# Output weights by column halves in a two-problem attention block

## The chip, the cores and the metric

The kernel runs on one core of one Trainium2 chip. A core has a matrix engine (TensorE, PE in the profile, with its weight loads shown apart as PEld), VectorE (DVE), ScalarE (ACT), GpSimd (POOL) and SyncE (SP), which here only issues transfers to the core's DMA engines. The metric is the device time of one execution in microseconds; lower is better. Before the change it is 728.03 us (median of 3 runs, 727.68 to 728.79).

## What is computed

Two independent problems A and B of the same shapes, each a grouped-query attention over a given key and value cache, followed by an output projection. Their outputs stand side by side.

```python
B, Sq, D = 16, 80, 576
Hq, Hkv, Sk, Dh = 32, 16, 512, 128          # bfloat16
def ref(x, k_cache, v_cache, wq, wo):
    q = (x @ wq).reshape(B, Sq, Hq, Dh).transpose(0, 2, 1, 3)
    k = jnp.repeat(k_cache, 2, axis=1)
    v = jnp.repeat(v_cache, 2, axis=1)
    scores = jnp.einsum("bhqd,bhkd->bhqk", q, k) * (Dh ** -0.5)
    o = jnp.einsum("bhqk,bhkd->bhqd", softmax(scores), v)
    return o.transpose(0, 2, 1, 3).reshape(B, Sq, Hq * Dh) @ wo
out = jnp.concatenate([ref(A...), ref(B...)], axis=-1)   # 16 x 80 x 1152
```

## The kernel before

**Tiling.** A unit is one batch entry with four key heads, that is eight query heads: an octet is the eight query heads over eight batch entries. There are 128 units, numbered U in the order in which they are worked on. Problem A comes first. Within a problem the octets come in pairs (`hh`, sixteen heads, `HH = 16`), and within a pair the batch comes in two halves (`half`), so that a stage of 32 units (one `prob`, one `hh`) holds sixteen heads of all 1280 rows. Two neighbouring units are the same batch entry in the two octets of the pair.

For each unit:

- TensorE projects queries (`em_qp`, L538, four matmuls of 320 columns, and the tail of the contraction, 576 - 512 rows, `em_qt`, L551). This runs 12 units ahead.
- TensorE forms scores: four blocks of 128 query rows (`em_qk`, L670, 512 columns each) and the residual 32 rows of each group (`em_qkr`, L657, four narrow matmuls per unit, two units together).
- VectorE takes each row's negated maximum (L679), ScalarE the exponential with its row sum (L683), VectorE the reciprocal (L689), GpSimd scales the row (L692).
- TensorE transposes the probabilities (`em_tr`, L724, 40 small matmuls, with the projection's tail ahead of them), and VectorE or ScalarE copies them out of PSUM into `pT` (L735 to L744).
- TensorE multiplies by V (`em_pv`, L767, four matmuls per key head), and VectorE or ScalarE copies the result into `oT` (L781), which holds a stage's attention output with the heads' width on the partitions.

**Output projection.** For each stage there are 20 output tiles: ten row tiles of 128 rows by two column halves of `DC = 288` (`NOC = 2`). An output tile is 16 matmuls into one PSUM bank, one per head, issued as two operations of eight (`em_op`, L816, `OPSPLIT = 2`), here called half tiles. In a problem's first stage the tile is copied to `acc` (L827); in the second it is added to `acc` into `osb` (L844) and stored (L850).

The output weights of a stage (`wo`, 2048 rows by 576) are loaded by SP in four transfers of four heads each (`em_ldwo`, L592), into one of four slots of `wo_sb`. All four go to one semaphore (`d_wo`). Each half tile reads all four slots and the `oT` of both octets:

```python
ot_reads = [R(("oT", half, b_, q_, pr_), ver) for b_ in bls for q_ in range(2) for pr_ in range(2)]
...
reads=ot_reads + [R(("wo", c_ % NWS), c_) for c_ in range(ci0, ci0 + NWC)]
```

**Order.** The kernel doesn't leave the order of its 5256 operations to a scheduler at run time. Every operation is registered with an engine, a key, what it reads and what it writes; operations of a kind form a stream (scores, PV, output half tiles `P`, K loads, `wo` loads and so on, 41 of them), in the order of their keys. The text `ORDER` then merges the streams: each letter takes the next operation of a stream, a quote mark ahead of it gives a copy out of PSUM to ScalarE and not to VectorE, and the digits behind it name the PSUM banks (0 to 7) that it takes. That merged order is the program order of every engine, and dependencies between engines become semaphore waits (`finalize`). So TensorE, VectorE, ScalarE, GpSimd and SP each run a fixed list and wait at its head.

**Queues and buffers.** All loads and stores stand in SP's list: K (L623, one transposing transfer for two units, three buffers of two units), V (L627, six buffers of one unit), `wq` and its tail (L503, L507), `wo` (L592), x and the stores of the output (L850, two buffers). A transfer at the head of SP's list that waits for its buffer holds back all that stand behind it. A K load waits for the last scores of the two units that used its buffer, a V load for the last PV, a `wo` load for the last half tile that read its slot, a store for its addition on VectorE.

Of the kernel before, what the change touches and what calls it, by code (L numbers as in the profile page):

```python
# [14 lines left out]
NK = 6  # L15
# [5 lines left out]
ILV = 0  # L21
VK = 8.0
KK = 8.0
NQ = 2
NWS = 4
NOC = 2
NOSB = 2
NWARM = 8
NWC = 4
# [19 lines left out]
OPSPLIT = 2  # L49
# [13 lines left out]
nEKni7KHHHHHNHj3j4IMj5Nj6MIMId3Ik4d5ILIk2dd4aBAd1dd3'ABEj5d4dd7AMd1LBdd3'Bd4dd6'ABAd2dd3BMd4Aadd5Ad6d'ABe0e1'B  # L63
oe2e7d3old4oldoe0'Bf6olf1d4p'AKe5ld2homKdpe3d7alod6lCBudAe0md2Cuoe5le4Ood1u'Boldvf36Alud0BlCd7Cpu'Adpv'Ag1245B
mue0we7'zouj1j3'yd5MulhMk4d1xhmoj3adMe0'BLe2log1346Cluc7xoe3'Acuoc0le5wolj1e2'yoe3'ze4oclc6CcMu'sof15lutd7lpvj
2e0lMc3pFcme2Fd4Cov'th'sog13FulCFue6xld0houa'BCe2'wCyd4'zu'Aoumg13ulc7ye5Oluok6c'wzuf12'Alxc0vpc'se3p'tc5e7'Bc
Lmoc0d4mse1oe6lce2Ctd5ulod3uColg07volb1uzluwe7y'Ad6oe2g04xlCBubo'yu'zCe0'xvc7ochc4u'shqc'wb5'BauAllf17e2pe6bCp
mvoc3mue0d1t'quCd7oluog45lulcxc6sc'w'Be2Ce0u'tod3'yvd6olzg47uh'Ahlc5hze1'wca'xo'ye0d7'Bsle2Ce6ouc4'Acoluf15tc3
lCcpud4'spmug02omvc3Czc'yue1e5'toe2ule0b3o'wlxod6lbBole1'qc4oe2lae5cold3Ac0locg17'tlf02z'se5'wCb4'yxuCp'A'Bvpe
1md6uoc7mchCuCe0o'sc3he2lvoche7hlbtuaolud3olug15'quf02y'zue4lpe5b1'wCCmxuod7'Bup'Ae0d3luoc6oculbv'sle6g45o'qCb  # L70
1uwlzu'xA'yc0c'Be7tme6c3oche0od4lad5Colug27Csluf36z'yue0Cc2xuwcoe7'Aub'tp'Bvlod4umqe2e0oc5vlcd3o'slpg17halc5wc
z'xe2'yd0Amoe1e7c4'Boc'td3lCsuc6olce2ug45'tolf16w'yCzub7'xlpue5'Bc4mvohce2he3'Aoblholc1pd5lscd2CCtve0g34auub1'
zxomuwbyluB'Ae6e4oc3cc5ole0d2s'qCcolvd3'qe7u'tf46olug15pGlCb0hwumChCxzv'yhe7b'Bouplue1c3Acud4oe2usd5lqug37ob1y
'w'zClue0e7oame3ubolxe2lqd6Coc1u'Acoc7luce0B'tc4scle1Cod3u'tolg57vvf24yld0uwx'Ae1pd5h'zpJmg67Jo'Bc2'yze3cmCc6x
uwe7slcac4oue2'Aco'Bc1ld0ocle5td3olg67tlse1C'ye2uoe4d5'zwu'xe6olb7ohlhe1oblCCBulc2oe4v'qcAald3uof07ulg16pv'sCc
4'wzumb2p'ye0Cxmcvoe1d6'tuo'Ae7c4luoe5blCBold3JCcJvc1'scGule0hg47ou't'qf15y'xuld2Bu'wpe4'ze0ud3'AComg67uplc1z'
ycc4C'xwe7'svocmac6d1Buloe5ue3'tcoc0lud4Alsuce2o'tg67olf05y'x'wb3lp'Aze6me2ob'Bple0Ce1Co'qe7uc4acoulc3cod6vltd
2ulog03use1mb4olwe5zblxCC'Boud3hCyue1lhe2d7hov'qc5h'Aocluhg46luf01'xu'sBc2'zcupd5'thy'we7me2b6oAle0oe4c3aod7lo
blCCulcg02su'qve6'zxc3oe4'ycb2Cltvoue0we6lobuo'Aule4Cd3pu'qd5BmuCog02luf17x'zyuc6'Bhcp'wue0'Ac5slce2ohe6mc3oad
4ltcd1Colug05slupe2'zvc3Cyc'w'xe6u'td5omc3uCBd0loucg17sluf23v'wz'x'yc6BchAe1'tc7phce0Cb4omuo'sue6lbovlAe1e2lod  # L80
5e0qld7oag46plb1xmwz'Ae2o'Be3c6'yd5ole7Cobuloulce0c4lochc3se2ctd7'tholg46CCCue3'yxb0uo'w'zuBe4lAe6c7uCalcod5vq
lc2ovcd3slutf14ug27ppme6bz'wmoe1b7ylhCoe4'qvb'Aouxd5CF'quBle0Fe2uod3lFoug67FlCuf14xlwBud0'zpe2u'ye3oc7'Acumc6o
cvd5'stle1CKug67olc2'yzcc3'wp'xcle7Cd6sv'Aoe1mc2ud0Bloucc4'ste5cloe2g37'tColf14Chylvb5a'zuCp'xe2u'Be7od3mue0ol
buo'wlud2rle1Aug57pc6y'zcd0'wo'se7b5loKme6Kbo'xalCBe1v'Ad4olue2c7Crlcuog36uCtlf15xuy'wc7'zcpu'Bc3e2scvme6oc7u'
tchoe1ld3Duolhd4sk2'Apg67lLd0'x'Be1y'zc2aco'wd4mCe7u'Ac6oc'tc3luse2cClog56uCtluf17y'zue3xe2'wob5u'Aplve0hobmho
hle6pd3Dlc1hoc'Bc2rd0Dcg45thsd2zmb1y'x'w'BCAle7vc4ocue0e6loae5ubColuc7sld3uoe0crlg46Cov'tCf15'wxu'zd7p'Bu'Ae6b
3'yuolpue2blCoume0ud4loDvg16hCrle2zmc3coe0b6aslxoe5'ye3bwB'AClove1d4olue0c7olcud5Colug23rlutf16y'xhu'we7'zCDe0
ouc2'Ac'Bc3Cvplcd4shumd5oDutg27lue1w'xc3'zCpe0vc'Aac7ymucd4o'tue2'soc7lucoe6d3lsc1'Bocle0tg57olf12Club6puhCwme
0hxubo'Bu'zAe1'yrd3plDd4oe7Gg56olc0Jw'yce1'zc5c'x'sd6th'Be0loJe5b4aCmouole7vboluAd2lre0c3ocg45'slf13z'yc7xcp'B
e5d4'twlCAe2uc7Comcub6Colve0'se1uohle5d7Duolbaovlpg02ulruc1C'wC'zce6u'xtd5'Ay'Bue1d4mCoug27olue0xb3lvwo'Auze1l  # L90
e6e5uohd7yd0lobKolc2Ccr'Bue1C'sf36olug24plupc5mucc1tc'zvc3hs'xe5'wDe4'yocJd1mtGd2loJe6Bc3Klcoc5K'Ace0D'stg47la
of35'ze6lb7o'yCxle0uwe4Cob'Bu'Aplue2oe1c6mvcrd0o'sud3lpg67lCvc4zmb2uo'xu'Be7le5ocbaolCe1C'wurd3loe2ud7'Aolug05
y'tulCf14xyv'zc6c'Bue0c5'soc'wue2'tc7hod6lhAclhd5CCpuD'sg03pume2yud7'zomk1vc3Ld0lue4c'x'wao'Bg12Ale5wc6o'ycc4'
# [174 lines left out]
def bass_concat_heads__gqa_block_cached__gqa_block_cached__near_ridge_kernel(  # L268
# [27 lines left out]
    with ExitStack() as es:  # L296
# [32 lines left out]
        def R(res, ver):  # L329
            return (res, ver)  # L330
# [598 lines left out]
```

## Time and profile before

| | |
|---|---|
| time, median of 3 runs (lowest to highest) | 728.03 us (727.68 to 728.79) |
| the profiled execution's own time | 731.59 us |
| its span, from the first to the last instruction | 729.8 us |
| mean granted clock of TensorE | 0.997 |
| HBM read, written | 87.65 MB, 2.95 MB |
| output half tiles' matmuls (L816) | 1280, 287 ns each from start to modelled end |
| `wo` loads | 16 of 576 KB, landing 4.0 to 9.2 us after issue |
| K loads | 64, landing 6.1 to 13.4 us after issue |

The profile is one execution, recorded instruction by instruction. Its groups are named by engine and by line of the kernel, with what is written and read (`ps<-wo_sb,oT` writes PSUM from the weights and the attention output). Matmuls are pipelined: the duration of one overlaps the next, so their spacing is read from the starts. "Idle before" and "waits" say what an engine stood for; the chain of waits follows the last instruction back to what released it at each step. A stretch is a window of time with each engine's busy time in it.

### The profile page before, as it was taken

Reading aid. Unit: us, or ns where it says so; the run is one execution under the profiler, and the core shown is the slowest. Engines: PE = TensorE matmul, PEld = TensorE weight load, DVE = VectorE, ACT = ScalarE, POOL = GpSimd, SP = SyncE. Lnnn points to the kernel's source line nnn. Section 1 sums busy time; section 2 is a strip of 40 time slices with the busy share of each in tenths; the row PEclk is TensorE's granted clock in tenths of the full one; section 3 lists DMA queues with packets and bytes.
Section 4 is the critical chain, followed back from the end, with each engine's and each line's share of the span. In section 5 each row is a group of like instructions: output and inputs, shape, how many; then the busy total and the mean of one; then the engine's idle time right before and its main releaser. Section 6 shows DMA issues by size and latency. Waiting matters only on the chain.

```text
span 729.8 us, 26289 instructions
## 1 busy us (share of the span) xinstructions
PE 719.5 (99%) x10820; PEld 514.5 (71%) x10820; DVE 637.6 (87%) x1447; ACT 643.9 (88%) x1856; POOL 432.0 (59%) x650
## 2 busy tenths in 40 slices
PE   9999999999899999999999999999999999999998
PEld 5567777777677777777777777777777777777677
DVE  4998898998799989889898987999888998989995
ACT  1999997998879989999899998899999999898993
POOL 0466656566637546646666575665755756757772
PEclk9999999999999999999999999999999999999999
DMA  9999998989979999999899994999978989897950
GB/s 235 257 282 253 247 229 231 213 208 243 221 176 258 209 247 241 260 212 229 205 235 243 271 250 124 249 232 253 207 188 204 259 190 223 203 240 191 207 165 19
DMA packets 365976, 160.73 MB, mean 220 GB/s; under 512 B 278560, under 2 KB 362784, under 8 KB 365856
## 3 DMA queue, kind: packets, MB, share of 16 engines
q1 hardware_dynamic: 365856, 159.05, 92.6%
q8 instruction: 86, 1.41, 0.8%
q14 instruction: 34, 0.28, 0.1%
HBM read 87.65 MB, written 2.95 MB: 124 GB/s over the span
## 4 chain that ended last, share of the span: by engine, by line
PE 87%; DMA 4%; ACT 3%; DVE 3%; SPq 1%; issue 1%; POOL 1%
PE ps L816 21%; PE ps L767 18%; PE ps L538 16%; PE ps L670 14%; PE ps L724 9%; PE ps L657 4%; PE ps L551 4%; DMA kT<-in_A_k_cache_dram 3%; ACT p_sb L683 3%; DVE negmax L679 2%; DMA kT<-in_B_k_cache_dram 1%; POOL p_sb L692 1%; SPq L503 1%; SPq L507 0%; ACT pT L735 0%
## 5 line engine op out<-in xcount | busy, mean ns | idle before, releaser
L692 POOL TENSOR_SCALAR p_sb<-p_sb,rinv 128x512 bf16<-128x512 bf16 x640 | 430.2, 692 | 282.2 <-DVE rinv L689 281.8
L683 ACT ACTIVATE p_sb<-ps,negmax 128x512 bf16<-128x512 f32 x640 | 442.2, 706 | 31.6 <-DVE negmax L679 25.5
L679 DVE TENSOR_REDUCE negmax<-ps 128x1 f32<-128x512 f32 x640 | 417.3, 680 | 37.2 <-PE ps L670 29.4
L767 PE MATMUL ps<-pT,v_sb 128*128 128x160 bf16 x2048 | 187.9, 233 | 2.3 <-issue 1.9
L816 PE MATMUL ps<-wo_sb,oT 128*128 128x288 bf16 x1280 | 182.9, 287 | 0.6 <-issue 0.4
L767 PEld LDWEIGHTS ps<-pT,v_sb 128*128 128x128 bf16 x2048 | 152.8, 98 | 40.0 <-issue 5.0
L670 PE MATMUL ps<-kT,qT 128*128 128x512 bf16 x512 | 175.5, 381 | 0.5 <-DMA kT<-in_A_k_cache_dram 0.3
L538 PE MATMUL ps<-xT,wq_sb 128*128 128x320 bf16 x1024 | 174.0, 299 | 0.3 <-DVE xT L402 0.3
L816 PEld LDWEIGHTS ps<-wo_sb,oT 128*128 128x128 bf16 x1280 | 122.4, 98 | 45.6 <-ACT p_sb L683 2.7
L683 ACT ACTIVATION_READ_ACCUMULATOR p_sb<-ps,negmax 128x1 f32 x640 | 141.3, 221 | 0.0
L538 PEld LDWEIGHTS ps<-xT,wq_sb 128*128 128x128 bf16 x1024 | 95.2, 98 | 44.3 <-ACT qT L564 1.6
L724 PEld LDWEIGHTS ps<-ident,p_sb 64*128 64x128 bf16 x5120 | 91.4, 95 | 9.3 <-ACT oT L781 1.9
L724 PE MATMUL ps<-ident,p_sb 64*128 64x64 bf16 x5120 | 95.8, 190 | 1.1 <-DVE oT L781 0.6
L735 ACT COPY pT<-ps 128x512 f32<-128x512 f32 x145 | 85.2, 600 | 12.2 <-PE ps L724 11.9
L737 DVE COPY pT<-ps 128x1024 bf16<-128x1024 bf16 x111 | 75.7, 685 | 12.0 <-PE ps L724 10.6
L564 ACT ACTIVATE qT<-ps 128x320 bf16<-128x320 f32 x156 | 69.0, 454 | 17.8 <-PE ps L551 15.5
L781 DVE CAST oT<-ps 128x320 bf16<-128x320 f32 x129 | 61.6, 481 | 10.2 <-PE ps L767 9.4
L670 PEld LDWEIGHTS ps<-kT,qT 128*128 128x128 bf16 x512 | 48.3, 98 | 26.5 <-ACT p_sb L683 4.8
L781 ACT CAST oT<-ps 128x320 bf16<-128x320 f32 x127 | 54.5, 440 | 10.0 <-PE ps L767 9.8
L565 DVE TENSOR_SCALAR qT<-ps 128x320 bf16<-128x320 f32 x100 | 47.2, 480 | 6.1 <-PE ps L551 4.5
L744 DVE COPY pT<-ps 128x256 bf16<-128x256 bf16 x135 | 36.7, 281 | 12.5 <-PE ps L724 11.0
L657 PE MATMUL ps<-kT,qT 128*32 128x512 bf16 x512 | 39.6, 384 | 0.9 <-DMA kT<-in_B_k_cache_dram 0.5
(31 smaller groups left out, 191.2 us busy)
## 6 DMA issues: line engine op xcount, KB each, us to landing
v_sb<-in_A_v_cache_dram SPq DMA_DIRECT2D x64, 512.0 KB, 5.3
v_sb<-in_B_v_cache_dram SPq DMA_DIRECT2D x64, 512.0 KB, 4.8
wo_sb<-in_A_wo_dram SPq DMA_DIRECT2D x8, 576.0 KB, 6.1
wo_sb<-in_B_wo_dram SPq DMA_DIRECT2D x8, 576.0 KB, 6.6
wq_sb<-in_B_wq_dram SPq DMA_DIRECT2D x4, 1024.0 KB, 6.3
out_dram<-osb SPq DMA_DIRECT2D x40, 72.0 KB, 3.7
wq_sb<-in_A_wq_dram SPq DMA_DIRECT2D x8, 256.0 KB, 4.6
wq_sb<-in_A_wq_dram SPq DMA_DIRECT2D x2, 1024.0 KB, 6.0
```

The costliest lines, as they stand in the source:

```text
L538: last = e.matmul(ps[:, vbq[h].phys, QO:QO + 320], lhsT=wq_sb[:, wsl, ck, hi * 128:(hi + 1) * 128], rhs=xT[:, half, ck, n0:n0 + 320], star ...
L564: return e.activation(dst, src, AF.Identity, scale=SCALE)
L670: return e.matmul(ps[:, vb.phys, :], lhsT=qT[:, qsl, bl, gl * 160:gl * 160 + 128], rhs=k_of(U, gl), start=True, stop=True)
L679: return e.tensor_reduce(negmax[:, si:si + 1], ps[:, vb.phys, :], axis=AX.X, op=AluOpType.max, negate=True)
L683: return e.activation(p_sb[:, psl, :], ps[:, vb.phys, :], AF.Exp, bias=negmax[:, si:si + 1], scale=1.0, accum_out=rowsum[:, ss, k:k + 1])
L692: return e.tensor_scalar(p_sb[:, psl, :], p_sb[:, psl, :], rinv[:, ss, k:k + 1], 1.0, op0=AluOpType.mult, op1=AluOpType.mult)
L724: last = e.matmul(dst, lhsT=p_sb[64 * h:64 * h + 64, psls[k_], j * 128:(j + 1) * 128], rhs=ident[64 * h:64 * h + 64, 64 * h:64 * h + 64], ...
L735: return e.copy(pT[:, pts, :, :].bitcast(F32)[:, :, 32 * h:32 * h + 32], ps[:, vtp[h].phys, :].rearrange("p (n c) -> p n c", n=16))
L737: return e.tensor_copy(pT[:, pts, :, 64 * h:64 * h + 64], psb[:, vtp[h].phys, :].rearrange("p (n c) -> p n c", n=16))
L767: last = e.matmul(ps[:, vo.phys, off:off + 160], lhsT=v_sb[:, vs, gl, j * 128:(j + 1) * 128], rhs=pT[:, pts, 4 * gl + j, :], start=(j == 0 ...
L781: return (e.copy if en == "act" else e.tensor_copy)(dst, src)
L816: last = e.matmul(ps[:, vb.phys, 0:DC], lhsT=oT[:, hi, rb * 128:(rb + 1) * 128], rhs=wo_sb[:, wi, c3 * DC:(c3 + 1) * DC], start=(hi == 0), ...
```

## The change

**Loads.** `wo_sb` becomes four buffers of eight heads by 288 columns, one for each pair of column half (`c3`) and octet. A stage's four transfers carry the same bytes as before, each with rows of 576 bytes and not 1152, and each has a semaphore of its own. The second column half's loads get a key that is five output tiles later than the first's.

**Tiles.** Output tiles go by column half: all five row tiles of a batch half with `c3 = 0`, then the five with `c3 = 1`. The last ten tiles of all keep the old order, row tile by row tile. A half tile is now the eight heads of one octet; it reads the `oT` of that octet and the one buffer of `wo` that it needs. A lower bound on a tile's key keeps it behind the PV of its last unit.

**Order.** `ORDER` is another text for the same 5256 operations, with the same number in each stream; the keys' constants `OPX`, `LP0` and `WOK` that sort the half tiles and `wo` loads change with it. Counted by transpositions (one per unit) that stand ahead of them, the four `wo` loads of the stages stand at 2, 2, 3, 3; 34, 34, 34, 35; 66, 66, 66, 67; 98, 98, 98, 99 before, and at 1, 3, 11, 11; 33, 34, 37, 42; 65, 69, 70, 73; 97, 97, 103, 103 after. Half tiles stood in groups of two to four between transpositions with gaps (ahead of transpositions 20 to 32 by count: 20, 22, 24, 24, 24, 26, 28, 30, 32, 32, 32, 34, 36), and now 20, 22, 22, 22, 23, 24, 25, 26, 28, 28, 29, 30, 32. Of the copies out of PSUM, ScalarE had 575 and VectorE 489; now ScalarE has 563 and VectorE 501.

The K load is rewritten with a constant `KSP = 0`, with which it issues the same transfers to the same places as before. The warm-up matmuls read other views of `wo_sb` of the same size.

```diff
@@ constants @@
-NWS = 4
-NWC = 4
-OPSPLIT = 2
+KSP = 0
-OPX = ((12.0, 1.8), (18.5, 1.45), (17.5, 1.05), (8.5, 1.35))
-LP0 = 8.5
+OPX = ((7.0, 1.6), (6.7, 1.7), (9.0, 1.7), (11.0, 1.35))
+LP0 = 11.0
+WOK = 6.0
@@ ORDER: all of it @@
...
@@ buffers @@
-        wo_sb = sb("wo_sb", [128, NWS * (HH // NWC), D], BF16)
+        wo_sb = sb("wo_sb", [128, 4, HH // 2, DC], BF16)
-        warm = wo_sb[:, 0, 0:512]
-        ones = wo_sb[:, 1, 0:128]
+        warm = wo_sb[:, 0, 0:2, 0:256]
+        ones = wo_sb[:, 0, 3, 0:128]
@@ loads of wo @@
-                for wc in range(NWC):
-                    h0 = hh * HH + wc * hc
-                    ci = (prob * NPAIR + hh) * NWC + wc
-                    wos = ci % NWS
-                    x = 5.0 * (prob * UPR + hh * NPP * 16 + OPX[2 * prob + hh][0]) - WOL * (NWC - wc)
+                for wos in range(4):
+                    c3, h0 = wos // 2, hh * HH + wos % 2 * (HH // 2)
+                    ci = prob * NPAIR + hh
+                    o0_, os_ = OPX[2 * prob + hh]
+                    x = 5.0 * (prob * UPR + hh * NPP * 16 + o0_ + c3 * os_ * NRT) - WOL * (2 - wos % 2) - WOK
...
-                        src = wo_ap[h0 * 128:(h0 + hc) * 128, :]
-                        return e.dma_start(wo_sb[:, wos * hc:(wos + 1) * hc, :],
-                                           src.rearrange("(h p) n -> p h n", p=128))
+                        src = wo_ap[h0 * 128:(h0 + HH // 2) * 128, c3 * DC:(c3 + 1) * DC]
+                        return e.dma_start(wo_sb[:, wos, :, :], src.rearrange("(h p) n -> p h n", p=128))
...
-                          dsem="d_wo", name="ldwo%d.%d.%d" % (prob, hh, wc), stream="wo")
+                          dsem="d_wo%d" % wos, name="ldwo%d.%d.%d" % (prob, hh, wos), stream="wo")
@@ output tiles @@
-                        r, c3 = divmod(n, NOC)
+                        r, c3 = divmod(n, NOC) if prob == 1 and hh == NPAIR - 1 and half == NPP - 1 else (n % NRT, n // NRT)
...
+                        x = max(x, 5.0 * (base + 16 * half + 2 * bls[-1] + 1) + PV0 + 4.0)
...
-                        ot_reads = [R(("oT", half, b_, q_, pr_), ver) for b_ in bls for q_ in range(2)
-                                    for pr_ in range(2)]
+                        ot_reads = [[R(("oT", half, b_, q_, pr_), ver) for b_ in bls for pr_ in range(2)] for q_ in range(2)]
...
-                                for hi in range(sp_ * hs, (sp_ + 1) * hs):
-                                    wi = (ci0 + hi // hc) % NWS * hc + hi % hc
-                                    last = e.matmul(ps[:, vb.phys, 0:DC], lhsT=oT[:, hi, rb * 128:(rb + 1) * 128],
-                                                    rhs=wo_sb[:, wi, c3 * DC:(c3 + 1) * DC],
-                                                    start=(hi == 0), stop=(hi == HH - 1))
+                                for i in range(HH // 2):
+                                    last = e.matmul(ps[:, vb.phys, 0:DC],
+                                                    lhsT=oT[:, sp_ * (HH // 2) + i, rb * 128:(rb + 1) * 128],
+                                                    rhs=wo_sb[:, 2 * c3 + sp_, i, :],
+                                                    start=(sp_ == i == 0), stop=(sp_ == 1 and i == HH // 2 - 1))
...
-                                  reads=ot_reads + [R(("wo", c_ % NWS), c_) for c_ in range(ci0, ci0 + NWC)],
+                                  reads=ot_reads[sp_] + [R(("wo", 2 * c3 + sp_), ci)],
```

More of the change, by code (lines that the diff above doesn't have):

```diff
@@ L67 @@
[L67 to L71, printed above, removed]
@@ new lines @@
+1md3Bo'tcmg45hF'se6'yxe1hCBc7u'zFe4oclae5vb3olute0lwboolc7Ce1olud6Acluc4qcCovd3se0ulg25Cou'tf17'yxuCBe4'zd2wvp
+lc3d5uAmoe0ucpg16'sulob3wlze4A'ye6bhCouholavc2d1q'xulcd3tme0Bf26og45plpc7mcyd0'wme2sc4oc'ze7d6C'txulBc4cou'Ae5
+c3'socle1g24o'thlChCe7uxb3'who'yua'Ae2le5uoe0b'zuolCe1Bd4ulod6vloc7ue2lCqcc5ovlcg03slCtvf17y'zue2'xCb3p'Buwmpc
+6ucAbmuo'sue0le1hoc7ud4'qhold3hae2lcCovg56'tluf01y'zub7w'xCpu'Be2Ambuople0c3oc'qc4'se2d5loce7C'td3vole0ug46lub
+2'zCymohb'wJxBGe1'qc7oJcle2hc3Ald4hoe0acClod5vsg16lu'tuf27C'zwyb3u'xpuc6AmcuBe0e1oe4uc5bsloc'qd6tle0od3oe1lg25
@@ L352, in em_warmend @@
         def em_warmend(e):
-            return e.memset(warm[:, 0:2], 0.0)
+            return e.memset(warm[:, 0, 0:2], 0.0)
         S.add("dve", -1000, em_warmset, writes=[R(("warm",), 0)], name="warmset", stream="warmset")
@@ L627, in em_ldv @@
                 return e.dma_start(v_sb[:, vs, :, :], src)
-            if goct < ILV or U % 2 == 0:
+            if kw == 1 or U % 2 == 0:
                 S.add("sp", 5.0 * gfirst[U] + 0.5 * (U - gfirst[U]) - LA - KK, em_ldk,
-                      writes=[R(("kT", (U + i_) % NK), U + i_) for i_ in range(2 if goct >= ILV else 1)],
+                      writes=[R(("kT", (U + i_) % NK), U + i_) for i_ in range(kw)],
                       dsem="d_k%d" % ks, name="ldk%d" % U, stream="K")
```

148 lines of the change are left out of this document (75 added, 73 removed).

## The prediction

> **What bounds the kernel now.** I read the page first, then the gaps between matmul starts, then who waits for whom, then stretches of time, then the DMA landings. The page says that TensorE hardly pauses, at full clock, while VectorE and ScalarE are close behind and the DMA engines are nearly full:
>
> ```profile
> span 729.8 us, 26289 instructions
> ...
> PE 719.5 (99%) x10820; PEld 514.5 (71%) x10820; DVE 637.6 (87%) x1447; ACT 643.9 (88%) x1856; POOL 432.0 (59%) x650
> ...
> PEclk9999999999999999999999999999999999999999
> ...
> q1 hardware_dynamic: 365856, 159.05, 92.6%
> ```
>
> Busy time of pipelined matmuls overlaps, so 99% proves little. I therefore laid the 10820 matmuls of the trace against the order table, operation by operation: 1664 TensorE operations, from the start of each to the start of the next. Medians: an output half tile (8 matmuls, L816) 0.980 us, a head of PV (4, L767) 0.277, a score block (L670) 0.216, a head's projection (4, L538) 0.543, a pair's residual scores (8, L657) 0.548, a transposition with projection tails (42, L724 and L551) 0.825, without tails 0.690, and about 0.096 more ahead of an operation that uses part of the array. Over before's table these medians add up to 712.7 us; the trace needs 724.8 from first to last start. So 12.1 us are waits, 11.1 of them in 39 gaps of over 0.04 us, the rest jitter. They lie in four places. Under 50 us: 2.7. From 194 to 201 us: 3.7. Elsewhere to 660 us: 2.0. From 666 to 693 us: 2.7. Rows for the second and the last:
>
> ```profile
> PE ps L767 <- issue: 1.9, 1, 1.9
> ...
> 197.00:200.40 3.40, 3.40 (x19) 0.50 0.74 190
> ...
> 672.00:692.00 20.00, 18.62 (x355) 12.91 (x348) 19.75 (x48) 19.93 (x59) 15.48 (x24) 1.00 0.97 214
> ```
>
> The first row is the longest wait of TensorE's matmuls, for nothing that the profile shows; the second (stretch, PE busy, granted clock) says that half the clock followed it. I count neither against the table's order, and the timed runs seem to lack the event: 731.6 less 3.7 is 727.9, against a median of 728.03. My baseline is **727.9**. The third row (PE, weight loads, DVE, ACT, POOL busy) shows VectorE and ScalarE full for 20 us while TensorE pauses: the 2.7 us near the end are theirs. In the chain of waits, two K loads decide:
>
> ```profile
> 321.25 10.14 DMA kT<-in_A_k_cache_dram
> ...
> 596.40 9.70 DMA kT<-in_B_k_cache_dram
> ```
>
> K pairs 29 and 54 landed 0.14 us before their first score block started; TensorE stood 0.52 and 0.60 us around them. That is 1.1 of the 2.0; the other 0.9 is scattered.
>
> **The change, part by part.**
>
> *TensorE work.* Every count stays: 160 half tiles, 512 PV heads, 512 score blocks, 256 projections, 128 transpositions. The medians summed over the new table (a dozen new neighbour pairs priced by their first member) give 711.9: **-0.8**. The half tiles' matmuls have the same 288 columns, and the four wo semaphores in place of one add waits ahead of them at no price: a score block followed by a half tile takes the same 0.216 us as one followed by another score block. The warm-up reads other views of the same buffer, as large as before: 0.
>
> *First eight heads don't wait for the second octet.* This wait costs nothing today: of the idle time before L816's operations the trace puts 0.4 us, in two waits, down to a copy into oT (L781); and the shortest distance from a PV to the half tile that needs it is 0.69 us by the medians (0.92 after). **0**, at best -0.4. Its loss is bounded by banks held longer (a tile's bank is open 2.5 us in the median before, 2.9 after, 7 at most in both), which is in the distances below.
>
> *wo in column halves.* Still 16 loads of 576 KB, each row of 576 bytes and not 1152:
>
> ```profile
> wo_sb<-in_A_wo_dram SPq DMA_DIRECT2D x8, 576.0 KB, 6.1
> ...
> SPq L850 <- DVE osb L844: 39.6, 13, 12.6
> ...
> SPq L592 <- PE ps L816: 3.4, 2, 2.5
> ```
>
> In the packet records 1152 bytes take 51 ns and 576 bytes (the output stores) 29, so 16384 x 29 - 8192 x 51 is 57 us over 16 engines: 3.6 us of DMA time, 0.5% of the span. K, V and wo lie ahead of need by several us, which hides it: **0**, at worst 3.6. The Trainium skill (DMA: Bandwidth & Descriptors, Specifications) has line rate from 512 bytes up, so by it there would be no loss at all; the trace disagrees, since 576 bytes in 29 ns is 19.9 bytes per ns against 22.6. By the page the worst case here would be 0.
>
> On SP's queue a wo load waits for the last reader of its buffer with K, V, weights and stores queued behind it; K in turn waits behind stores, which stood 39.6 us at the head for their VectorE add (pair 53 was issued 0.4 us after one). Before: four wo loads in a row, 3.4 us of waiting. After, on the medians' clock, 13 us over the six that wait at all, the longest 5.4. What decides is how long before its use each K pair is issued, counting everything ahead of it on SP (4.5 us per K, 0.4 to 0.6 per other load, from SP's rows). Before: lowest 7.5 (pair 53), 9.0 (54), 10.9, 12.3 (29), 12.3. After: 10.0 (pair 60), 11.2 (62), 11.8 (63), 12.0 (56), 12.8 (34), 13.3 (40). K lands 8.1 us after issue in the middle, 9.4 to 10.1 in the waits above. So both of today's waits go and pair 60 may come just late: 1.1 becomes 0.5, **-0.6** (between -1.1 and the third case below). The wo loads themselves gain distance: first use 10.5 to 13.2 us after issue today in the last three stages, 22 to 59 after, but one at 10.3; the longest landing is 9.2.
>
> *Even output tiles.* VectorE's and ScalarE's work per 20 us of TensorE's (rows' means; 0.645 for a max and 0.67 for an exponential, as these follow one another in the chain): before, mostly 17 to 21 in each, but 25.2 and 24.4 in the last full stretch but one, just where the third row above has both full. After, the largest are 22.4 and 22.3 (600 to 620), and 22.3 and 22.8 from 40 to 60, where before has 19.0 and 19.7. The tight places near the end go: before, units 121 and 122 have 4.6 and 5.0 us from last score to transposition, and banks come round after 1.36 (scores), 0.58 and 0.65 (PV) where the waits are; after, the shortest are 5.3 (the last unit; 5.1 there before, without a wait), 1.90 and 0.76, besides a transposition's bank at 0.55. So of 2.7 I leave 0.4: **-2.3**, between -2.7 and 0. At the start I take 2.7 to 3.0, **+0.3** (0 to +3): projection work ahead of the first scores is longer (the first K landed at 18.9 us, now first needed at 18.1 by the medians plus 1.2 for the first start), but x is loaded ahead of the second K pair, which had 3.9 us to spare, and the first transposition stands 5.8 us behind its residual scores, 7.6 before. For 600 to 620 add **+0.1**. The end after the last tile (3.8 us from its first matmul) keeps its order.
>
> *Sum:* 727.9 - 0.8 - 0.6 - 2.3 + 0.3 + 0.1 = **724.6**. Waits left: 4.9 of today's 7.4 (the event at 194 us left out). No waits at all would give 727.9 - 0.8 - 7.4 = 719.7.
>
> **Rivals.**
>
> *Waits move but don't shrink.* VectorE and ScalarE carry 22 us of work per 20 in two new stretches; if the 2.4 us too much stay in each (as before's 5 too much left 2.7, a half), 2 x 1.2 comes on top, and with pair 60 late by another 0.5 it is 727.5: within 0.2% of 728.03, which is about what a measurement here can tell from none (1.5 us). For: all three engines stand within 13% of full. Against: a queue a few operations deep spreads a bump, and before's stretch of 20.5 and 23.0 at 60 to 80 us cost 0. This is also the case in which the change does not do what it says, as its third part frees nothing.
>
> *K comes late.* The second pair of wo loads now lands amid K and V, and in the last units K's distances are the shortest. K has been slower where wo loads lay beside it:
>
> ```profile
> DMA to landing us min/median/max: 6.1/8.1/13.4
> ```
>
> The 13.4 is pair 4, issued just behind four wo loads at the start. Landings as slow at 10.0, 11.2, 11.8, 12.0, 12.8 and 13.3 would cost 3.4 + 2.2 + 1.6 + 1.4 + 0.6 + 0.1 = 9.3, 8.8 over my 0.5: **733.4**, slower. It decides from 12.6 us on (2.6 + 1.4 + 0.8 + 0.6 = 5.4, which gives 729.5). Against: K lies at 6 to 10 us once the start is over, and few weights are loaded near the end. As the row at 197 us stands after a stop of 2.0 us, each stop that long may cost 1.7 more at half the clock, so two would end at 736.8. The Trainium skill (TensorE: Matmul & The Clock Gate, What's actually happening) has the clock fall only after an idle window of about 3.4 us; the trace agrees with the window's length (3.40 us at 0.50) but not with that need, as 2.0 us of idle was enough. By the page the stops alone would count: 733.4.
>
> **How the numbers follow.** Forecast 0.68, waits that move 0.20, late K 0.12. Likeliest time 724.6; its own range 721.5 to 726.6. Faster by over 0.2% means under 726.6: 0.68. Within: 0.20. Slower, over 729.5: 0.12. The range runs from 721.5 (hardly any wait left, plus jitter) to 729.3, so that the late K's upper part is left out.
>
> **What would show it.** Starts of TensorE's operations should again add up to about 712, with 5 us of waits on top. The stretch that ends 40 us before the end should have VectorE and ScalarE under 19 of 20. No K load should stand as a long piece in the chain after 60 us, except perhaps pair 60. wo rows should land in 6 to 9 us in pairs. I am wrong if waits past 2 us appear ahead of L657 or L670 on a K load, if ScalarE or VectorE is full for 20 us where TensorE pauses, or if half-tile matmuls start over 0.123 us apart.

## The result and the profile after

The changed kernel takes 722.53 us (median of 4 runs, 721.79 to 722.56) where the kernel before takes 727.93 (4 runs, 727.68 to 728.79). The ratio is 0.9921, with a 95% interval of 0.9904 to 0.9938: faster by 5.4 us in the medians, 4.5 to 7.0 by the interval. The profiled execution is one of 722.56 us. Line numbers differ from kernel to kernel: the score block, the exponential, PV, its copy and the addition into `osb` are L670, L683, L767, L781 and L844 before, L673, L686, L770, L784 and L845 after, and up to 9 lines further down than before in experiments 1, 2 and 4. The lines of the page that answer to those shown of before, with the first line of the chain of waits:

```profile
span 720.6 us, 26290 instructions
...
PE 715.3 (99%) x10820; PEld 513.1 (71%) x10820; DVE 641.3 (89%) x1459; ACT 639.8 (89%) x1844; POOL 432.6 (60%) x650
...
q1 hardware_dynamic: 374048, 159.05, 95.6%
...
PE 98%; ACT 1%; issue 0%; DVE 0%
...
wo_sb<-in_A_wo_dram SPq DMA_DIRECT2D x8, 576.0 KB, 5.6
```

The busy shares hardly move. What moved is the chain: its line gives TensorE 98% of the span, and no K load is in it. The same line of before:

```profile
PE 87%; DMA 4%; ACT 3%; DVE 3%; SPq 1%; issue 1%; POOL 1%
```

Problem A's wo lands 0.5 us sooner (6.1 before), although it comes in twice as many packets. SP's waits, the rows that answer to the two of before (total us, times, longest):

```profile
SPq L851 <- DVE osb L845: 35.1, 10, 8.9
...
SPq L590 <- PE ps L673: 9.4, 4, 4.6
```

The wo loads do stand longer at the head of SP's list (9.4 us here against 3.4). All the same, K came in time: the landings, and five stretches of time (PE, weight loads, DVE, ACT, POOL busy, the granted clock, DMA share, GB/s; a share above 1.00 means that the recorded times of packets overlap).

```profile
DMA to landing us min/median/max: 6.3/8.6/13.1
```

```profile
20.00:40.00 20.00, 19.34 (x234) 11.57 (x234) 19.91 (x46) 19.99 (x60) 11.51 (x19) 1.00 1.15 270
40.00:60.00 20.00, 20.00 (x353) 13.93 (x351) 19.98 (x47) 20.00 (x62) 14.11 (x22) 1.00 1.11 272
600.00:620.00 20.00, 20.00 (x323) 13.90 (x322) 19.50 (x42) 19.87 (x62) 13.37 (x20) 1.00 0.91 195
660.60:680.60 20.00, 20.00 (x323) 14.72 (x321) 18.68 (x43) 18.30 (x56) 16.17 (x24) 1.00 0.88 187
680.60:700.60 20.00, 20.00 (x324) 14.47 (x323) 18.79 (x45) 19.92 (x59) 13.54 (x21) 1.00 0.80 222
```

In the second and third stretch VectorE and ScalarE are as full as they were at 672 to 692 us before, and TensorE does not pause; in the first they are as full, and it does (one wait of 0.7 us at 27 us). So two full engines alone are not reason enough for a pause. The fourth is the stretch that ends 40 us before the end: both engines are under 19 of 20, as the prediction had asked. In the fifth ScalarE is full again, without a pause.

Laid against the order table as in the prediction, TensorE's operations take 715.6 us from the first start to the last (724.8 before). "Medians" is the sum of undisturbed spacings, "waits" what stands above them, by place in the kernel. The last two rows are experiments told below.

| profile | time, us | first to last start | medians | waits under 50 us | 50 to 640 | behind 640 |
|---|---|---|---|---|---|---|
| before | 731.59 | 724.8 | 712.0 | 3.3 | 5.6 | 2.7 |
| after | 722.56 | 715.6 | 711.5 | 1.2 | 1.4 | 0.0 |
| before, a quarter of V | 725.48 | 718.8 | 712.0 | 3.2 | 0.4 | 2.0 |
| after, a quarter of V | 721.42 | 714.5 | 711.5 | 1.3 | 0.2 | 0.0 |

The time is the first-to-last distance plus 6.7 to 7.0 us in each row. So the gain lies in waits, in all three places, and 0.5 us of it in spacings. Two things about the first row. Its medians are not those of the prediction: taken from before's profile alone they are 712.7, with 2.7 us of waits under 50 us, so some 0.6 us can be booked as spacing or as waits at the start (after alone has 711.3 and 1.2). And the profiled execution of before is 3.6 us above its median time, because the event at 194 us is at its longest there and half the clock follows it. Experiment 1, with the same order and bank numbers and the same time, has 2.3 us in the middle column by the same working; with that figure the waits that went are 2.1, 0.9 and 2.7 us, and with 0.5 of spacings the sum is 6.2, near the 5.4 between the medians.

### The profile page after: what moved, and what is told of

The parts are those of the page before. It is cut to its first block, busy times and chain, and to the rows that moved or that the text cites. A ratio compares the mean times of both kernels' runs of the same rounds, so it can differ in the third digit from the quotient of the medians.

```text
span 720.6 us, 26290 instructions
## 1 busy us (share of the span) xinstructions
PE 715.3 (99%) x10820; PEld 513.1 (71%) x10820; DVE 641.3 (89%) x1459; ACT 639.8 (89%) x1844; POOL 432.6 (60%) x650
## 4 chain that ended last, share of the span: by engine, by line
PE 98%; ACT 1%; issue 0%; DVE 0%
PE ps L816 22%; PE ps L770 20%; PE ps L537 19%; PE ps L673 16%; PE ps L727 11%; PE ps L660 5%; PE ps L550 4%; ACT p_sb L686 1%; PE ps L348 0%; PE ps L396 0%; ACT qT L563 0%; PE ps L414 0%; PE ps L451 0%; DVE osb L845 0%; DVE wo_sb L341 0%
## 5 line engine op out<-in xcount | busy, mean ns | idle before, releaser
L686 ACT ACTIVATE p_sb<-ps,negmax 128x512 bf16<-128x512 f32 x640 | 444.0, 711 | 29.8 <-DVE negmax L682 25.5
L770 PE MATMUL ps<-pT,v_sb 128*128 128x160 bf16 x2048 | 191.1, 233 | 0.1
L770 PEld LDWEIGHTS ps<-pT,v_sb 128*128 128x128 bf16 x2048 | 154.0, 98 | 39.5 <-ACT pT L745 3.3
L673 PE MATMUL ps<-kT,qT 128*128 128x512 bf16 x512 | 176.4, 381 | 0.0
L537 PE MATMUL ps<-xT,wq_sb 128*128 128x320 bf16 x1024 | 176.0, 299 | 0.0
L686 ACT ACTIVATION_READ_ACCUMULATOR p_sb<-ps,negmax 128x1 f32 x640 | 144.0, 225 | 0.0
L738 ACT COPY pT<-ps 128x512 f32<-128x512 f32 x150 | 88.4, 603 | 9.4 <-PE ps L727 9.0
L740 DVE COPY pT<-ps 128x1024 bf16<-128x1024 bf16 x106 | 72.0, 684 | 13.2 <-PE ps L727 11.7
L563 ACT ACTIVATE qT<-ps 128x320 bf16<-128x320 f32 x131 | 59.5, 462 | 16.2 <-PE ps L550 15.4
L784 DVE CAST oT<-ps 128x320 bf16<-128x320 f32 x129 | 61.5, 482 | 6.5 <-PE ps L770 6.0
L564 DVE TENSOR_SCALAR qT<-ps 128x320 bf16<-128x320 f32 x125 | 59.5, 482 | 8.1 <-PE ps L550 6.6
L673 PEld LDWEIGHTS ps<-kT,qT 128*128 128x128 bf16 x512 | 48.4, 97 | 25.7 <-issue 3.3
L784 ACT CAST oT<-ps 128x320 bf16<-128x320 f32 x127 | 56.4, 448 | 10.2 <-PE ps L770 9.9
L745 ACT COPY pT<-ps 128x128 f32<-128x128 f32 x132 | 36.1, 288 | 7.0 <-PE ps L727 6.8
L692 DVE RECIPROCAL rinv<-rowsum 128x3 f32<-128x3 f32 (+1 forms) x256 | 39.5, 161 | 2.3 <-ACT p_sb L686 2.2
```

Source lines behind the costliest of these rows:

```text
L537: last = e.matmul(ps[:, vbq[h].phys, QO:QO + 320], lhsT=wq_sb[:, wsl, ck, hi * 128:(hi + 1) * 128], rhs=xT[:, half, ck, n0:n0 + 320], star ...
L563: return e.activation(dst, src, AF.Identity, scale=SCALE)
L673: return e.matmul(ps[:, vb.phys, :], lhsT=qT[:, qsl, bl, gl * 160:gl * 160 + 128], rhs=k_of(U, gl), start=True, stop=True)
L686: return e.activation(p_sb[:, psl, :], ps[:, vb.phys, :], AF.Exp, bias=negmax[:, si:si + 1], scale=1.0, accum_out=rowsum[:, ss, k:k + 1])
L738: return e.copy(pT[:, pts, :, :].bitcast(F32)[:, :, 32 * h:32 * h + 32], ps[:, vtp[h].phys, :].rearrange("p (n c) -> p n c", n=16))
L740: return e.tensor_copy(pT[:, pts, :, 64 * h:64 * h + 64], psb[:, vtp[h].phys, :].rearrange("p (n c) -> p n c", n=16))
```

## The experiments

Each was timed in several rounds beside the kernel before on the same chip (728.4 to 728.7 us there).

**1. The layout alone.** Before's table to the letter, with wo in column halves, four semaphores, and half tiles that wait for both octets and all four buffers.

```diff
 # ORDER, tile order and wo keys: before's
-        wo_sb = sb("wo_sb", [128, NWS * (HH // NWC), D], BF16)
+        wo_sb = sb("wo_sb", [128, 4, HH // 2, DC], BF16)
-                                  reads=ot_reads + [R(("wo", c_ % NWS), c_) for c_ in range(ci0, ci0 + NWC)],
+                                  reads=ot_reads[0] + ot_reads[1] + [R(("wo", w_), ci) for w_ in range(4)],
```

> Before's order and tiles, with wo loaded by column halves (rows of 576 bytes) into four buffers; each half tile still waits for all four buffers and both octets. Theory (the halved rows are hidden, the gain is all in the order): same as before, 728 us within 1; wo packets 16384 of 576 bytes, DMA share up by 0.5 to 3% of the span. Rival (the separate buffers themselves help): under 726.5. Rival (the shorter rows cost DMA time that is not hidden): up to 3.6 us slower, 731.5, with K loads landing after TensorE asks for them in more than the two places of before.

Measured: 728.70 us, ratio 1.0002 (0.9988 to 1.0015). The queue's row on its page:

```profile
q1 hardware_dynamic: 374048, 159.05, 92.6%
```

The 8192 more packets are there, and the share of time is 92.6%, as before. The layout is worth nothing and costs nothing, to within 1 us.

**2. The end alone.** Before's table up to transposition 107, the changed order from there. The kernel around it has the new buffers, and each half tile reads its own octet and one buffer, as after.

```diff
 # ORDER
-<before: 128 transpositions>
+<before: to transposition 107><after: the rest>
```

> Before's order up to transposition 107, then after's order for the rest; wo by column halves, tiles row by row. Theory (VectorE and ScalarE overload near the end is 2.7 us of the gain): waits past 660 us fall from 2.7 to about 0.5, a seam at transposition 107 costs up to 0.8, TensorE's medians add up to 0.5 less: 728.0 - 2.2 - 0.5 + 0.5 = 725.8. Rival (the gain lies in the loads and the early stages): 727.5 to 728.

Measured: 728.24 us, ratio 0.9996 (0.9986 to 1.0006). The expectation missed. Waits of TensorE from 605 us on, all that the profile names:

```profile
PE ps L679 <- ACT qT L567: 0.7, 1, 0.7
PE ps L679 <- DVE qT L568: 0.5, 1, 0.5
PE ps L679 <- DVE pT L746: 0.2, 1, 0.2
```

None lies behind 640 us, so the end's 2.7 us did go. But these waits stand at 615 to 634 us, where the two orders were joined (2.3 us with the smaller ones; on the medians one bank came round there 0.2 us after its last matmul). A seam cut by hand costs as much as the thing under test, so this run decides nothing by its time.

**3. VectorE relieved at the end.** Before's kernel, with the row maximum of units 112 to 122 taken over 128 of the 512 columns.

```diff
-                def em_max(e, vb=vb, si=si):
-                    return e.tensor_reduce(negmax[:, si:si + 1], ps[:, vb.phys, :], axis=AX.X,
+                def em_max(e, vb=vb, si=si, nc_=128 if 112 <= U <= 122 else 512):
+                    return e.tensor_reduce(negmax[:, si:si + 1], ps[:, vb.phys, 0:nc_], axis=AX.X,
```

> Before, with the row maximum of units 112 to 122 taken over the first 128 of 512 score columns, which takes some 0.4 us off each of 55 VectorE operations there and leaves order, banks and ScalarE alone. Theory (VectorE full for 20 us is what holds TensorE near the end): waits past 660 us fall from 2.7 to under 1.2, time 726 to 726.8. Rival (ScalarE, equally full, or the short way round of the PSUM banks holds it): waits stay over 2, time 727.5 to 728.

Measured: 728.05 us, ratio 1.0000 (0.9988 to 1.0012). The stretch of the prediction's third row, and TensorE's waits from 660 to 700 us, of this kernel:

```profile
672.00:692.00 20.00, 18.80 (x344) 13.09 (x340) 13.51 (x48) 20.00 (x59) 15.71 (x25) 1.00 0.97 220
```

```profile
PE ps L724 <- ACT oT L781: 0.8, 2, 0.6
PE ps L816 <- issue: 0.4, 1, 0.4
PE ps L816 <- ACT p_sb L683: 0.3, 1, 0.3
```

The rows of before that answer to the first of these:

```profile
PE ps L724 <- DVE oT L781: 0.6, 1, 0.6
...
PE ps L724 <- ACT oT L781: 0.3, 1, 0.3
```

VectorE falls from 19.75 to 13.51 of 20, and the waits stay at 2.55 us (2.66), operation by operation: 0.65 ahead of transposition 120 in both. A full VectorE was not their cause. The "issue" row is told of below. What the others wait for are copies out of the banks that they take (L781 copies PV's result, L683 is a score's exponential), soon after the matmuls that filled them. The longest, ahead of transposition 120, can be followed to its end. In both kernels the transposition takes the bank of the first two PV heads of unit 118, and the copy that frees it is ScalarE's; the VectorE copy that the row of before names is of another bank and ended 0.04 us later. ScalarE in this run (start, us taken):

```profile
686.51 0.76 ACT L683 ACTIVATE p_sb<-ps,negmax 128x512 bf16<-128x512 f32 x1
...
687.17 0.51 ACT L781 CAST oT<-ps 128x320 bf16<-128x320 f32 x1
```

The bank's last matmul ended at 686.60, the copy began only behind the exponential ahead of it in ScalarE's list, and TensorE went on at 687.74, 0.06 us after the copy's end. The other waits of over 0.1 us in this stretch, the "issue" one left out, end the same way, on an operation of ScalarE's that began when the one ahead of it was done. So this run, which relieves VectorE alone, says nothing against ScalarE, which is full here too (20.00) and was relieved in no run.

**4. The start alone.** The changed order up to about transposition 4, before's from there, in the same kernel as experiment 2.

```diff
 # ORDER
-<before: 128 transpositions>
+<after: to transposition 4><before: the rest>
```

> After's order up to about transposition 4 (two wo loads there instead of four), then before's order; wo by column halves. Theory (the start is worth 1.2 us: waits before 50 us 2.7 in before, 1.5 in after, and 0.3 less in medians): 728.0 - 1.5 = 726.5, with the seam's 0 to 0.5 on top. Rival (the start is worth nothing, the difference there is one run's chance): 728.

Measured: 727.78 us, ratio 0.9989 (0.9980 to 0.9997), a smaller gain than the 726.5 expected. The waits under 52 us are 3.6 in sum, of which 1.3 (0.83 at 48.9 us, 0.48 at 51.3) are the seam; 2.3 without it, against 3.3. The gain that the ratio shows, 0.2 to 1.5 us, is the part that the seam left.

**5. The octet wait given back.** The changed kernel, each half tile waiting for both octets.

```diff
-                                  reads=ot_reads[sp_] + [R(("wo", 2 * c3 + sp_), ci)],
+                                  reads=ot_reads[0] + ot_reads[1] + [R(("wo", 2 * c3 + sp_), ci)],
 # ORDER: 22 first halves moved to just ahead of their second halves
```

> The changed kernel, in which every half tile waits again for the attention output of both octets. So that this can be met, 22 of the 80 first halves are moved to just ahead of their second halves, and PSUM banks are chosen anew there. On the medians some ten banks are then taken again 0 to 1.3 us after their last matmul, where the changed kernel has 0.76 or more. Theory: the wait of one octet for the other was worth nothing in before's order, but without its removal the changed order can't keep its bank distances; each of the ten short returns costs 0.2 to 0.7 us, together some 4 us: 726.5. Rival (the octet wait is worthless in either order): 722.5, within 0.7.

Measured: 739.88 us, 17.3 above the changed kernel and 1.0152 (1.0138 to 1.0166) of before. Waits of TensorE behind 50 us, the largest groups:

```profile
PE ps L673 <- ACT p_sb L686: 2.0, 5, 0.8
PE ps L537 <- ACT pT L738: 1.9, 3, 0.8
```

The direction was the theory's, the size four times its figure: 55 waits (20.7 us) and not ten. Where a first half of 0.98 us is taken out, everything behind it comes 0.98 us nearer to the operation whose bank it takes. Other than the expectation says, the order that ran keeps every bank number; besides the 22 moves only one copy near the end stands elsewhere. The wait and the moves were not separated, and another order might meet the wait for less.

**6. Before's end put back.** The changed kernel up to transposition 117, before's order to the end, no bank chosen anew; one store moved up.

```diff
 # ORDER
-<after: 128 transpositions>
+<after: to transposition 117><before: the rest>
```

> The changed kernel's order up to transposition 117, and before's order from there to the end; the weights' column halves stay, and no bank is chosen anew. Theory: before's waits near the end are short returns of PSUM banks written in its order (on the medians the banks of T119 come round 0.58 us after the last matmul on them, those of SR62 1.36, those of T120 0.65). So 1.8 to 2.3 us of TensorE waits come back behind 683 us, in the same places: 724.6. Rival (they come from what was queued up on VectorE and ScalarE before): no wait over 0.2 us past 683 us, 722.5.

Measured: 726.58 us, ratio 0.9968 (0.9955 to 0.9980). Waits of TensorE from 660 to 700 us, then stretches:

```profile
PE ps L770 <- DVE osb L845: 2.3, 1, 2.3
PE ps L673 <- ACT p_sb L686: 0.7, 1, 0.7
PE ps L727 <- ACT oT L784: 0.4, 1, 0.4
PE ps L727 <- DVE oT L784: 0.2, 1, 0.2
```

```profile
674.00:677.60 3.60, 1.40 (x45) 0.87 (x43) 1.00 (x4) 0.78 (x2) 0.55 (x1) 1.00 0.87 201
677.60:681.00 3.40, 3.31 (x51) 2.32 (x51) 3.10 (x10) 2.42 (x7) 2.59 (x4) 0.53 0.00 0
```

The first wait and 0.84 us just ahead of it are the seam (VectorE stood 2.6 us for a store, as two additions into one output buffer now follow closely), and half the clock for 3.4 us came behind it. The last two rows are before's short returns: transposition 120 waits 0.43 us (0.65 before), transposition 121 0.18 (0.19 before). They came back with the order, 0.6 us where the theory had 1.8 to 2.3; a sum of 2 us can't be read off this run, because the half clock lies over two of them, and the time answers to neither theory (724.6 and 722.5).

**7. Bank numbers only.** Before's order letter for letter; 289 of its bank numbers chosen so that the distance from a bank's last matmul to its next is as long as can be where it was shortest.

```diff
 # ORDER, its second line (the letters are the same)
-oe2e7d3old4oldoe0'Bf6olf1d4p'AKe5ld2homKdpe3d7alod6lCBudAe0md2Cuoe5le4Ood1u'Boldvf36Alud0BlCd7Cpu'Adpv'Ag1245B
+oe2e4d3old7oldoe0'Bf6olf1d5p'AKe2ld4homKdpe3d7alod6lCBudAe0md2Cuoe5le4Ood3u'Boldvf16Alud0BlCd7Cpu'Adpv'Ag5243B
```

> Before's kernel and order, letter for letter, with only 289 of its PSUM bank numbers chosen anew so that a bank comes round later where it came round soonest. On the medians the shortfalls against the shortest return without a wait fall from 12.8 to 5.5 us in sum (0.1 us of margin each). Near the end nothing else can be chosen (T119, SR62, T120 stay short). Theory: waits at the start shrink from 3.1-3.3 to about 2.2 and scattered ones by some 0.3; those past 660 us stay at 2.0 plus one of instruction fetch: 727.0. Rival (the numbers of banks don't matter, only which engine is full): 728.2, all waits as before.

Measured: 755.42 us, ratio 1.0368 (1.0352 to 1.0383): 27 us slower where a gain of 1 was expected. Waits of TensorE, the largest groups:

```profile
PE ps L670 <- ACT p_sb L683: 5.3, 11, 0.8
PE ps L767 <- ACT p_sb L683: 2.1, 5, 0.6
PE ps L657 <- ACT p_sb L683: 1.9, 4, 0.7
```

Neither theory had this. The shortest distances had become longer, as meant, and the waits went from 11.6 to 34.7 us in sum. They end on ScalarE's exponentials. I had taken one needed distance for all score banks, 1.95 us, near the shortest that went without a wait; but a bank is free when its copy is done, and that depends on the copy's turn in ScalarE's list. (That this is the whole reason is read from the waits; numbers chosen by the copies' ends were not tried.) With TensorE's work, the order and every engine's work the same, bank numbers alone moved 27 us.

**8 and 9. A quarter of V.** Both kernels, with V in full for the first six units only.

```diff
-            def em_ldv(e, vc_ap=vc_ap, b=b, q=q, vs=vs):
-                src = vc_ap[b, 4 * q:4 * q + 4, :, :].rearrange("g (p j) d -> p g (j d)", j=4)
-                return e.dma_start(v_sb[:, vs, :, :], src)
+            def em_ldv(e, vc_ap=vc_ap, b=b, q=q, vs=vs, w=4 if U < NV else 1):
+                src = vc_ap[b, 4 * q:4 * q + w, :, :].rearrange("g (p j) d -> p g (j d)", j=4)
+                return e.dma_start(v_sb[:, vs, 0:w, :], src)
```

> Before's kernel with V loaded in full for the first six units only, and after that only one of the four key heads' V; the other three multiply by V that an earlier unit left. This leaves out some 48 MB... that is 122 of 128 units times three quarters of 512 KB, about 46 MB of the 88 read. All engines have the same work. Theory: the long landings of K and the late instruction fetches come from full DMA queues, so the wait at 194 us (0.7 to 2.05 us and sometimes 3.4 us of half clock behind it), the ones at 545 and 692 us and those ahead of K pairs 29 and 54 go; the start (some 3) and the bank returns near the end (2.0) stay: 712 + 5.5 of waits + 0.8 jitter + 6.9 outside = 725.2. Rival (the wait at 194 us belongs to a place in the program, whatever the queues carry): it stays at 0.7 to 2, 727.

> The changed kernel with V loaded in full for the first six units only, and after that one of the four key heads' V; the other three multiply by V that an earlier unit left (about 46 MB of 88 are not read). All engines have the same work. Theory: what is left of the changed kernel's waits behind 50 us (three of 0.3 to 0.5 us, 1.3 in sum) are instruction fetches behind full DMA queues, and go: 721.3, with waits only under 50 us (1.2). So in both kernels the waits on the DMA queues are 1 to 3 us and the changed kernel keeps a lead of some 4 us over before's with the same quarter of V (725.48). Rival (the changed kernel's gain was mostly in what the DMA queues carry): the two with a quarter of V come out within 1.5 us of each other, 724 to 725.

Measured: before 725.48 us, ratio 0.9957 (0.9944 to 0.9970); after 721.02, ratio 0.9897 (0.9885 to 0.9910). Both came within 0.3 us of the theory. To read why, the event at 194 us first, in the DMA queues of the kernel before (queue: packets, MB, share), the stretch 188.8 to 194.1 us and then 194.1 to 196.6:

```profile
q1 hardware_dynamic: 4412, 1.51, 112.9%
```

```profile
q1 hardware_dynamic: 487, 0.32, 93.4%
q8 instruction: 1, 0.02, 2.8%
```

Queue q8 brings TensorE its own instructions: 86 packets of 16 KB for the 21,985 of the trace, one for each 256. A block of 256 lasts about 8 us. The packet for the next one starts 2.05 us (median) after the current one begins, and the next begins no sooner than 2.2 to 2.6 us after that start. Here the block began at 188.7 us with the rings full of K and V; the first row has no packet of q8, and the second shows the one that was due. It started 5.5 us after its block's begin and not 2, and TensorE stood 2.05 us in the middle of a PV, "for nothing that the profile shows". Then the stretch from 186 to 204 us of before with a quarter of V:

```profile
186.00:204.00 18.00, 18.00 (x268) 13.28 (x266) 17.26 (x38) 16.77 (x50) 9.19 (x15) 1.00 0.61 133
```

TensorE does not stop there at a DMA share of 0.61. The same wait, at the same count of TensorE's instructions, stood in the five other profiles that have before's order and bank numbers in that place (experiments 1 to 4 and 11), between 0.70 and 2.05 us. That it belongs to a block's border shows in the counts: before's three stops of this kind come ahead of instructions 5569, 16321 and 20929, after's ahead of 2753, 5057 and 5313, and all six lie whole blocks of 256 apart. And after, with a quarter of V, all of TensorE's waits that the profile names:

```profile
PE ps L348 <- DVE wo_sb L341: 1.2, 1, 1.2
PE ps L727 <- ACT qT L563: 0.7, 1, 0.7
```

The first is the warm-up's start, the second a bank at 27 us. So the waits that go with three quarters of V are worth 3.1 us (0.43%) in before, to about 1 us, and 1.7 (0.24%) in the changed kernel, to about 1.5; 4.4 us (0.60%, to about 1.3 us) of the distance between the two stays without them. By the table's rows that is 1.9 at the start, 2.0 at the end, and 0.5 in spacings.

**10. Before's start put back.** Before's order up to transposition 2, the changed order from there.

```diff
 # ORDER
-<after: 128 transpositions>
+<before: to transposition 2><after: the rest>
```

> The changed kernel with before's order up to transposition 2 (the first 34 us), and the changed order from there; no bank is chosen anew. Theory: of the changed kernel's gain some 2 us are made under 50 us, where before's table has short bank returns (waits 3.1 to 3.3 us against 1.2); they come back: 724.5, with waits of 3 us under 50 us. Rival (the start is worth nothing in time, because the wait for the first K only moves): 722.5.

Measured: 724.29 us, ratio 0.9943 (0.9931 to 0.9956), within 0.2 of the theory. The waits under 50 us are 4.4, of which a seam takes 1.7 (the first row below, and 0.48 at 48.5 us). Seven of the eight short waits of before's start, 0.17 to 0.38 us each, are back: with the first loads 2.8 us, against 1.2. So the right total holds a seam too; what the run's waits show for the start itself is 1.6 us.

```profile
PE ps L414 <- POOL acc L383: 1.0, 1, 1.0
PE ps L537 <- ACT p_sb L686: 0.3, 1, 0.3
```

**11. K first.** Before's kernel, three K pairs earlier in SP's list.

```diff
 # ORDER, SP's part
-... st8 wt6 wq3 wt7 x8 x9 st9 K29 ... st20 K53 V105 V106 st21 K54
+... K29 st8 wt6 wq3 wt7 x8 x9 st9 ... K53 st20 K54 V105 V106 st21
```

> Before's kernel with K pair 29 moved ahead of seven transfers in SP's list (stores, wq, x), pair 53 ahead of one store and pair 54 ahead of a store and two V. Nothing else changes. Theory: the waits ahead of K pairs 29 and 54 (0.52 and 0.60 us in before's profile) go, the one at 194 us stays, as it does not depend on them: 1.0 us less than before on the same chip, 727.3 to 727.7. Rival (they are not K's lateness but late instruction fetches or short banks at the same places): waits of 0.5 us stay at about 321 and 596 us, no gain.

Measured: 730.79 us, ratio 1.0035 (1.0022 to 1.0048), slower. The waits ahead of pairs 29 and 54 did go. In their place, TensorE at 327 us, and what VectorE waited for at that time:

```profile
PE ps L670 <- DVE osb L844: 2.2, 1, 2.2
```

```profile
DVE osb L844 <- DMA out_dram<-osb: 2.5, 1, 2.5
```

A K load that waits for its buffer now stands ahead of store 8; the output buffer came free late, VectorE stood at its next addition, and with it all maxima behind that. In SP's list a place for one transfer is taken from another.

**12. Less work for TensorE.** The changed kernel, seven of eight heads in each output half tile.

```diff
-                                for i in range(HH // 2):
+                                for i in range(1, HH // 2):
```

> The changed kernel with seven matmuls in each output half tile in place of eight: one head in eight is left out of the output projection, 160 matmuls or 19.6 us of TensorE's work. Theory: the order is cut to TensorE's pace; VectorE and ScalarE are busy 89% each and their copies can't come 2.7% sooner everywhere, so a part of the 19.6 us turns into waits for banks: 706 to 710. Rival (TensorE alone bounds, the others have room): 703.

Measured: 710.39 us. Of 19.6 us taken from TensorE 12.1 reached the time, 0.4 us outside the theory's 706 to 710; waits rose from 2.6 to 8.2 us, in 77 places of 0.1 us on the mean, and the other 1.9 us show as no wait. TensorE sets the time after the change too, but once 2.7% of its work is gone, 1% of the time is waits.

## Why the prediction was right, and where it was not

The forecast of 724.6 us had the sign and was 2.1 too slow; its sum has one term with the wrong sign, one reason that held by half and one baseline that was right by accident.

- **Baseline 727.9: the number held (727.93), the reason fell.** I left the event at 194 us out, as not belonging to the order and lacking in timed runs. It is in six profiles of before's order with whole V, with 0.70 to 2.05 us of wait, and is gone when the DMA queues are relieved. What four of the six lack is the 1.7 us of half clock behind it.
- **TensorE work -0.8:** -0.5 by the table's medians, -1.4 by those of each profile alone. The half tiles' matmuls kept their time (286 ns, 287 before).
- **Octet wait 0:** right for before's order. Experiments 2 and 4 have before's order over most of the kernel without that wait: the 0.4 us on copies into oT stay, and experiment 4's waits behind 52 us are 2.2 up to 640 us and 2.7 behind, against 2.3 and 2.7 with the wait (experiment 1). The new order uses that the wait is gone: with the wait and the moves made for it, it takes 17.3 us more. The step priced the wait and not what its removal lets the order do.
- **wo in column halves 0, at worst 3.6:** 0 within 1 us (experiment 1). The estimate of 3.6 us of more DMA time was not there in the share either.
- **K waits -0.6:** both went (1.1 us), and pair 60, feared just late, had 1.06 us to spare at a landing of 8.8. Against before's profile the term was too small. But how much of it is the new order's doing is open: with before's order and the new buffers, the wait ahead of pair 29 is in none of the profiles of experiments 1, 2 and 4, and that ahead of pair 54 in one (0.43 us). The view of SP's queue, with everything ahead of a K counted, found the pair that came nearest to being late; in experiment 11 moving K ahead, as it was moved there, cost more than it gave.
- **Even tiles, end -2.3:** the size was right, 2.7 measured, of which 2.0 stand with a quarter of V too; the reason that came first, VectorE and ScalarE full, failed for VectorE (experiment 3). For ScalarE it holds in part: the copies that TensorE waited for stood in ScalarE's list, but a full ScalarE makes no wait by itself (the stretches at 40, 600 and 680 us after). The second reason, that the short distances between a bank's last matmul and its next go, points at the right places: waits on just these banks' copies were there before, are gone after, and two of them came back with before's order (experiment 6). As a measure it failed in experiment 7: it counts TensorE's side only. What the traces show is the two together, a bank that is asked for early while its copy waits its turn in ScalarE's list; no run relieved ScalarE or moved only those copies. That the figure holds although half of its first reason fell is in part luck.
- **Start +0.3: the wrong sign, -2.0** (-1.5 by each profile's own medians, 1.6 in experiment 10). This is nearly the whole miss. I read the start by K, x and the first transposition, and what lies there are eight waits of 0.17 to 0.38 us between 29 and 44 us, most where the table brings a bank round early (on the medians 0.28 us after the last matmul at the shortest); the new order has one of 0.69. The distances had been weighed for the end and not for the start.
- **600 to 620, +0.1:** nothing. **Waits left 4.9:** 2.6.
- **Waits that move:** both stretches are full in the new profile and TensorE is busy 20.00 of 20 in each, so the price of 1.2 us each was wrong. One of the signs that the prediction set against itself, full engines where TensorE pauses, did appear, but at 20 to 40 us, and for 0.7 us. **Late K:** landings got no better (8.6 us in the middle), but the distances sufficed everywhere. The half clock behind a stop, which that rival used, is real and not certain (below).

## What to carry to other kernels

In this tuned order TensorE waited where a PSUM bank's reader got its turn too late, and how full the reading engine was over 20 us did not tell where. List the waits by bank and by the copy that frees it, at the start as much as at the end, and move work in between there. And a wait "for nothing" in the middle of one operation can be the engine's instructions: see whether such waits lie whole blocks of instructions apart, and what the transfers do at that moment.

## What was not expected of the hardware

TensorE's instructions come in over the DMA queues during the run, 86 packets here, and can be late when the loads fill those queues. Late packets of 256 instructions cost 0.3 to 2.05 us each in three places of before and three of after. They hit operations that wait for no data; in before's order the longest falls on the same count of instructions in six profiles, while in the changed order they are not in every run (experiment 6, which has that order up to 670 us, shows 0.1 us of waits from 50 to 200 us, where the changed kernel's own profile has 1.3).

After a stop of some 2 us the clock may fall, but need not: 1.9 us (the profile's figure, before and experiment 3) and 2.3 us (experiment 6) were followed by about 0.5 for 3.4 us; 1.6 and 2.2 us (experiment 11) by 1.00. The Trainium skill (TensorE: Matmul & The Clock Gate, What's actually happening) asks for an idle window of about 3.4 us first; the shorter stops that brought the lower clock here disagree.

Bank numbers, with all else equal, moved the time from 728.7 to 755.4 us (experiment 7).
